# New written orders for all five engines of an attention and MoE kernel, on one core

## The chip, the core and the metric

One core of one Trainium2 chip runs the whole program. The metric is the time of one execution on the device in microseconds. The core has five engines with queues of their own: TensorE (PE), VectorE (DVE), ScalarE (ACT), GpSimd (POOL) and SyncE (SP). SP here only issues transfers; POOL and ACT issue some too. Each engine runs its own queue in order, and engines wait for each other through semaphores.

## What is computed

```python
q_bits = (np.einsum('bhsd,dk->bhsk', q, proj) > 0)          # 6 bits per row, k likewise
mask = q_bucket[:, :, :, None] == k_bucket[:, :, None, :]   # same bucket of 64
scores = np.where(mask, scale * q @ k^T, -1e9)
attn = np.exp(scores - max);  attn = attn / (attn.sum(-1) + 1e-9)
x = (attn @ v) -> (1536, 512)                               # 2 x 8 heads, 768 x 64 each
h = x @ w_in;  x = (h - np.tanh(h)) @ w_out                 # 512 -> 2048 -> 512
g = x @ w_gate;  val = x @ w_val                            # 512 -> 1536
out = (g * sigmoid(g) * val) @ w_out2                       # 1536 -> 512
```

The weights of the MoE layers come as 64-bit numbers and are turned into 32-bit ones on the chip.

## The kernel before

**Attention.** Eight pairs of heads are worked on in 12 steps each, 96 steps in all. A step takes 128 query rows of one head against all 768 keys: PE multiplies the scores into one of two score buffers `s` (L838, four matmuls of 384 columns; now and then with a one-hot matmul of the buckets ahead of it, L835), DVE takes the maximum (L848), ACT the exponential with the row sum `sm` (L850), DVE or POOL adds 1e-9 (L854), DVE takes the reciprocal `r` (L856), and POOL multiplies the 768 columns of `p` by it (L857). PE transposes `p` in two halves of three blocks (L868), and ACT or DVE copies each half out of its bank `t` into `pt` (L874). After six steps, PE multiplies `pt` by `v` in two halves (PV, L891). The scores of step n+2 need the score buffer that the exponential of step n reads. Four buffers each of `p`, `sm` and `r` go round. Hash products (L801), the splitting of the next pair's q and k into a high and a low part (L660 to L662, L757, L758), and the moves of these by SP (L748) run beside it. The program's first steps have a form of their own: ACT and POOL split and scale the first pair (L660, L662), DVE adds (L686), ACT loads its function table ahead of a one-element exponential (`warm`, L1171).

**MoE layers.** Both layers multiply 2 x 2 blocks with seven products in place of eight. A unit is 256 columns of weights by 768 rows: seven product groups of six matmuls of 384 columns (L1047). Four of a unit's banks are emptied by ACT's copy, a snap (L1027), or by DVE's add of such a copy (L1030); then come tanh or sigmoid on ACT, DVE's or POOL's subtractions and products (L964) and ACT's rounding to a high part (L969). Product banks are called `bs`, and `t`, `x` and `h` go round. An output group is six matmuls (L1101): of 384 columns in layer 1, of 512 in layer 2. It is copied to `ct` or `acc` by ACT or DVE (L1132) and added up by an accumulating transfer from POOL's queue (L1140 in layer 1, L1149 to the output in layer 2); the last two blocks of layer 2 load that sum back (L1123, SP), and DVE adds to it (L1126). A weight chunk is loaded by SP (L463), converted on DVE (L465, L468, L471), combined (L497, L499: DVE or POOL), and split by ACT (L477, L514) and DVE or POOL (L479, L516).

**What sets the order.** The code declares 3381 operations, each with what it reads and writes and with the engines that can run it; an operation's number is its place in this declaration. `ORDER` is a table with one list of numbers for each engine, and `Plan.order()` walks all five lists: an operation goes to the engine in whose list it stands, and an engine's next instruction is the next number of its list. Where an operation can run on two engines, the list in which it stands is thus the choice:

```python
op({"DVE": 0.17, "POOL": 0.3}, lambda g: g.tensor_scalar(            # L854
    out=r, in0=sm, scalar1=1e-9, scalar2=None, op0=ALU.add), r=[smk], w=[rk])
op({"ACT": 0.4, "DVE": 0.47}, lambda g, dst=dst, src=src:            # L873
   g.activation(out=dst, in_=src, func=ACTF.Copy) if g is nc.scalar else g.tensor_copy(dst, src),
   r=[("t", z)], w=[ptk + (qt, z)])
tt: op({"DVE": dve(TB), "POOL": pool(TB)} if port else {"DVE": ...}, ...)   # L964
```

Of the kernel before, what the change touches and what calls it, by code (L numbers as in the profile page):

```python
# [46 lines left out]
def chunk_keys():  # L47
# [5 lines left out]
    for i in range(NP2):  # L53
# [51 lines left out]
    """,  # L105
    DVE="""
# [1196 lines left out]
```

## Time and profile before

| | us |
|---|---|
| median of three runs | 764.66 (762.88 to 764.97) |
| the profiled execution | 764.34 |
| its span on the core | 762.3 |
| PE busy | 744.4 (98%) |
| DVE busy | 601.5 (79%) |
| ACT busy | 451.6 (59%) |
| POOL busy | 354.1 (46%) |

The granted clock is at full speed over the span. Some 2 us lie outside the span. The attention takes the first 230 us, the MoE layers the rest, and the last matmul starts at 757 us. In the rows below a time is in microseconds from the start of the span unless it is a mean or a duration marked ns. A timeline row has the start, the duration, the engine, the line and the operation, with the idle time of the engine before it and who ended it in brackets. Durations of neighbours overlap, since engines pipeline; the distance from start to start is what a step takes on its engine.

### The profile page before, as it was taken

To read this page: it belongs to the slowest core of one execution; us is meant where nothing else is said; L and a number is where in the kernel's file an instruction comes from. 1 tells how busy PE (TensorE), PEld (TensorE's weight loads), DVE (VectorE), ACT (ScalarE), POOL (GpSimd) and SP (SyncE) were. 2 spreads that over 40 slices of the span, in tenths; PEclk is the share of its full clock that TensorE was granted. 3 is DMA by queue.
4 is the path that set the end of the run, shared out by engine and by line. 5 is a ranking of instruction groups with operands and counts; after the bars stand their busy time and mean duration, and the time that the engine had idled before them with its cause. 6 is when DMAs were issued, how large, how long until landed. Compare 5 with 4: busy or idle time off the path is not lost.

```text
span 762.3 us, 12361 instructions
## 1 busy us (share of the span) xinstructions
PE 744.4 (98%) x4342; PEld 656.0 (86%) x4342; DVE 601.5 (79%) x1077; ACT 451.6 (59%) x955; POOL 354.1 (46%) x390
## 2 busy tenths in 40 slices
PE   8899999999989999999999999999999999999997
PEld 4666676766668999999999999999999998999996
DVE  6879778889888578878677789997785767789465
ACT  5787898878876556555455456665455444454230
POOL 4665667877783843123135353734235544323010
PEclk9999999999999999999999999999999999999999
DMA  6564466357123036787575764323348565587304
GB/s 173 135 191 98 128 176 167 108 131 203 52 87 108 28 68 167 180 184 191 116 186 123 203 135 106 84 97 101 108 152 194 138 130 135 127 189 160 76 15 151
DMA packets 37245, 101.09 MB, mean 133 GB/s; under 512 B 4656, under 2 KB 10160, under 8 KB 37184
## 3 DMA queue, kind: packets, MB, share of 16 engines
q1 hardware_dynamic: 28288, 71.06, 30.6%
q0 software_dynamic: 8432, 28.45, 21.2%
q10 hardware_dynamic: 464, 0.80, 0.5%
q8 instruction: 34, 0.56, 0.3%
q14 instruction: 27, 0.22, 0.1%
HBM read 49.17 MB, written 15.73 MB: 85 GB/s over the span
## 4 chain that ended last, share of the span: by engine, by line
PE 81%; POOL 6%; DVE 6%; issue 2%; DMA 2%; ACT 2%; SPq 0%; POOLq 0%; DVEq 0%; ACTq 0%
PE bs L1047 30%; PE t L1101 16%; PE h L1101 8%; PE x L891 6%; PE s L838 6%; PE x L1101 6%; PE t L868 3%; PE x L1047 2%; POOL p L857 2%; PE t L1047 2%; DVE m L848 1%; ACT p L850 1%; DMA raw<-in_kT 1%; POOL x L555 1%; PE h L1047 1%
## 5 line engine op out<-in xcount | busy, mean ns | idle before, releaser
L1047 PE MATMUL bs<-x,wi 128*128 128x384 f32 x1200 | 230.7, 335 | 1.3 <-DVE p L1030 1.3
L1047 PEld LDWEIGHTS bs<-x,wi 128*128 128x128 f32 x1200 | 210.5, 188 | 6.1 <-DVE p L1030 1.6
L857 POOL TENSOR_SCALAR p<-p,r 128x768 f32<-128x768 f32 x96 | 94.6, 989 | 25.5 <-DVE r L856 15.5
L848 DVE TENSOR_REDUCE m<-s 128x1 f32<-128x768 f32 x96 | 90.8, 952 | 14.3 <-PE s L838 13.5
L850 ACT ACTIVATE p<-s,m 128x768 f32<-128x768 f32 x96 | 86.6, 903 | 20.2 <-DVE m L848 12.1
L838 PE MATMUL s<-op 128*128 128x384 f32 x384 | 91.9, 363 | 5.1 <-ACT p L850 4.8
L1027 ACT ACTIVATE p<-bs 128x384 f32<-128x384 f32 x120 | 57.0, 490 | 54.1 <-PE bs L1047 52.7
L838 PEld LDWEIGHTS s<-op 128*128 128x128 f32 x384 | 63.7, 189 | 21.6 <-ACT p L850 12.7
L868 PEld LDWEIGHTS t<-ident,pr 128*128 128x128 f32 x576 | 59.1, 140 | 22.9 <-POOL p L857 8.0
L1101 PE MATMUL t<-op,wo 128*128 128x384 f32 x384 | 75.8, 335 | 0.0
L874 ACT ACTIVATE pt<-t 128x384 f32<-128x384 f32 x133 | 61.2, 489 | 17.7 <-PE t L868 17.2
L868 PE MATMUL t<-ident,pr 128*128 128x128 f32 x576 | 64.9, 245 | 5.5 <-POOL p L857 3.2
L891 PE MATMUL x<-pt,v 128*64 128x384 f32 x384 | 69.0, 495 | 0.0
L1101 PEld LDWEIGHTS t<-op,wo 128*128 128x128 f32 x384 | 67.2, 188 | 0.7 <-DVE ct L1132 0.3
L1101 PE MATMUL t<-wo,op 128*128 128x512 f32 x264 | 67.1, 393 | 0.0
L1140 POOL DMA_DIRECT2D acc<-ct x24 | 21.0, 887 | 78.4 <-ACT ct L1132 32.2
L1101 PEld LDWEIGHTS t<-wo,op 128*128 128x128 f32 x264 | 49.0, 188 | 8.3
L479 POOL TENSOR_TENSOR wi<-fs,wi 128x512 fp32r<-128x512 f32 (+1 forms) x25 | 39.8, 1593 | 26.0 <-ACT wi L477 25.3
L477 ACT ACTIVATE wi<-fs 128x512 fp32r<-128x512 f32 (+1 forms) x60 | 41.9, 701 | 12.5 <-DVE fs L497 4.4
L1047 PE MATMUL bs<-op,wi 128*128 128x384 f32 x240 | 47.2, 335 | 0.5 <-DVE ct L964 0.5
L891 PEld LDWEIGHTS x<-pt,v 128*64 128x64 f32 x384 | 24.7, 136 | 25.9 <-issue 23.9
L1047 PEld LDWEIGHTS bs<-op,wi 128*128 128x128 f32 x240 | 42.1, 188 | 1.4 <-DVE ct L964 1.0
(186 smaller groups left out, 1385.8 us busy)
## 6 DMA issues: line engine op xcount, KB each, us to landing
raw<-in_w SPq DMA_DIRECT2D x68, 512.0 KB, 3.6
acc<-ct POOLq DMA_DIRECT2D x24, 768.0 KB, 6.3
out<-acc POOLq DMA_DIRECT2D x12, 768.0 KB, 8.3
op<-raw SPq DMA_DIRECT2D x42, 192.0 KB, 3.2
op<-f SPq DMA_DIRECT2D x56, 96.0 KB, 3.2
v<-in_v SPq DMA_DIRECT2D x8, 384.0 KB, 3.9
out<-acc SPq DMA_DIRECT2D x4, 768.0 KB, 4.6
acc<-out SPq DMA_DIRECT2D x4, 768.0 KB, 5.3
```

What stands on the lines that cost most here:

```text
L477: op({"ACT": act(n)}, lambda e: e.activation(out=hi, in_=src, func=ACTF.Copy), r=rk, w=[wk + (0,)], due=due, late=late)
L479: op({"POOL": pool(n), "DVE": dve(n)}, lambda e: e.tensor_tensor(out=lo, in0=src, in1=hi.bitcast(F32), op=ALU.subtract), r=rk + [wk + (0,) ...
L838: g.matmul(out=s[:, kh, 0:TB], lhsT=(b, a)[first][:, q0], rhs=ks[kh][0 if first else 1], start=first, stop=not first,)
L848: op({"DVE": 0.87}, lambda g: g.tensor_reduce(out=m, in_=sv, axis=AX.XY, op=ALU.max, negate=True), r=[sk + (0,), sk + (1,)], w=[mk])
L850: op({"ACT": 0.9}, lambda g: g.activation(out=p.rearrange("p (a b) -> p a b", a=2), in_=sv, func=ACTF.Exp, bias=m, accum_out=sm), r=[sk + ...
L857: op({"POOL": 0.91}, lambda g: g.tensor_scalar(out=p, in0=p, scalar1=r, scalar2=1.0, op0=ALU.mult, op1=ALU.mult), r=[pk, rk], w=[pk])
L868: g.transpose(out=t_t[z][:, kt * 128:(kt + 1) * 128].bitcast(F32R), in_=pr[:, z * TB + kt * 128:z * TB + (kt + 1) * 128], identity=ident)
L874: g.activation(out=dst, in_=src, func=ACTF.Copy) if g is nc.scalar else g.tensor_copy(dst, src),
L891: g.matmul(out=x[r, :], lhsT=v[:, kt, r], rhs=pt_t[ptks[e][1]][:, kt, :], start=(kt == 0), stop=(kt == NKT - 1), tile_position=(0, 64 * e),)
L1027: op({"ACT": act(TB)}, lambda e: e.activation(out=dst, in_=bank(), func=ACTF.Copy), r=[bk], w=dk, due=due)
L1047: e.matmul(out=bank(), lhsT=w[:, wpart, wi * 256 + k * 128:wi * 256 + k * 128 + 128], rhs=x_at(sb, xn, xpart, k), start=first and m == 0, ...
L1101: e.matmul(out=ps(), lhsT=lhs, rhs=rhs, start=c == 0, stop=c == 5)
```

## The change

Only the table `ORDER` is written anew; everything below it is the same, 17 lines further down. So L854 of before is L871 after, L857 is L874, L1047 is L1064, L1101 is L1118.

```diff
 ORDER = {e: [int(n) for n in t.split()] for e, t in dict(
     PE="""
-        7 17 8 19 24 28 32 37 58 44 39 48 68 78 104 88 52 64 66 106 74 76 116 84 139 86 149 94 96 161 112 114
...
+        7 17 8 19 24 28 32 37 58 68 48 44 39 52 78 104 88 64 66 106 74 76 116 139 86 84 149 96 94 161
...
     ACT="""
-        0 11 12 16 15 5 29 25 22 31 27 45 40 47 60 51 70 80 65 67 90 75 77 108 129 133 118 87 141 160 159 95 151
...
+        0 11 12 16 15 25 35 27 31 22 49 45 40 60 47 51 70 55 53 80 65 67 90 77 75 108 133 129 118 87 141
...
```

The engines chosen anew, in operations of each line:

| line (before) | what | before | after |
|---|---|---|---|
| L854 | add 1e-9 to the row sum | POOL 70, DVE 26 | POOL 19, DVE 77 |
| L873 | copies of transposed halves | ACT 133, DVE 59 | ACT 118, DVE 74 |
| L757 | high part of q and k | POOL 13, ACT 1 | POOL 9, ACT 5 |
| L479 | low part of in-weights | POOL 25, DVE 35 | POOL 10, DVE 50 |
| L497 | sums of weight blocks | POOL 37, DVE 23 | POOL 7, DVE 53 |
| L516 | low part of out-weights | POOL 13, DVE 15 | POOL 2, DVE 26 |
| L555, L560 | blocks of layer 2's input | POOL 11, DVE 22 | POOL 3, DVE 30 |
| L964 | subtractions and products | POOL 53, DVE 219 | POOL 11, DVE 261 |
| L1110, L1131 | copies of output groups | ACT 106, DVE 54 | ACT 84, DVE 76 |

On POOL at the start of the attention, where `r` and `p` of four steps go round (`r_159` and `p0_87` are those of every fourth step, the next step has `r_160` and `p1_88`), there stood before:

```order
L662 TENSOR_SCALAR f_75<-fs_71 128x768
L854 TENSOR_SCALAR r_159<-sm_152 128x1
L854 TENSOR_SCALAR r_160<-sm_153 128x1
L857 TENSOR_SCALAR p3_90<-p3_90,r_162 128x768
L857 TENSOR_SCALAR p0_87<-p0_87,r_159 128x768
L857 TENSOR_SCALAR p1_88<-p1_88,r_160 128x768
L854 TENSOR_SCALAR r_161<-sm_154 128x1
L854 TENSOR_SCALAR r_159<-sm_152 128x1
L854 TENSOR_SCALAR r_162<-sm_155 128x1
L857 TENSOR_SCALAR p2_89<-p2_89,r_161 128x768
```

and there stands now, at the same place:

```order
L874 TENSOR_SCALAR p2_89<-p2_89,r_161 128x768
L871 TENSOR_SCALAR r_162<-sm_155 128x1
L874 TENSOR_SCALAR p3_90<-p3_90,r_162 128x768
L871 TENSOR_SCALAR r_161<-sm_154 128x1
L874 TENSOR_SCALAR p0_87<-p0_87,r_159 128x768
L874 TENSOR_SCALAR p2_89<-p2_89,r_161 128x768
L874 TENSOR_SCALAR p1_88<-p1_88,r_160 128x768
L874 TENSOR_SCALAR p3_90<-p3_90,r_162 128x768
```

Most adds have left POOL's queue for DVE's, and multiplies stand next to each other.

On ACT at the program's start, with the semaphores that each instruction waits for (DMAHW3 is the transfer of the first half of k into `raw`), before:

```order
L638 DMA q<-in_qT 64x768 [waits DMAHW0_49]
L1171 ACT_TABLE_LOAD
L1171 ACTIVATE warm<-warm 128x1 [waits Pool_49]
L660 ACTIVATE op<-raw 128x384 [waits DMAHW3_49,DMAHW1_49]
L660 ACTIVATE op<-raw 128x384
L660 ACTIVATE op<-f 64x384 [waits DMAHW4_49]
L689 ACTIVATE op<-s_121,csb 64x384 [waits DMASW0_49,PE_49]
```

and now:

```order
L655 DMA q<-in_qT 64x768 [waits DMAHW0_49]
L677 ACT_TABLE_LOAD [waits DMAHW3_49]
L677 ACTIVATE op<-raw 128x384 [waits DMAHW1_49]
L677 ACTIVATE op<-f 64x384 [waits DMAHW4_49]
L706 ACTIVATE op<-s_121,csb 64x384 [waits DMASW0_49,PE_49]
```

The warm-up has moved to a place some 400 operations later on ACT; the table load now belongs to the first scaling and waits for its transfer.

On PE near the end of layer 2 (`bs`, `x_108`, `t` and `h_112` are the banks, `wo` an output weight, `op_86` the slots of the middle activations), before:

```order
L1047 MATMUL bs00_2415<-x1_2606,wi_63 128x384 x6
L1101 MATMUL t_116<-wo_81,op_86 128x512 x3
L1101 MATMUL t_116<-wo_82,op_86 128x512 x3
L1047 MATMUL bs01_2419<-x1_2606,wi_63 128x384 x6
L1101 MATMUL t_117<-wo_81,op_86 128x512 x3
L1101 MATMUL t_117<-wo_82,op_86 128x512 x3
L1047 MATMUL bs00_2415<-x1_2606,wi_63 128x384 x6
L1101 MATMUL x_108<-wo_81,op_86 128x512 x3
L1101 MATMUL x_108<-wo_82,op_86 128x512 x3
```

and now:

```order
L1064 MATMUL bs00_2415<-x1_2620,wi_63 128x384 x6
L1064 MATMUL x_108<-op_86,wi_63 128x384 x6
L1064 MATMUL bs00_2415<-op_86,wi_62 128x384 x6
L1118 MATMUL t_116<-wo_81,op_86 128x512 x3
L1118 MATMUL t_116<-wo_82,op_86 128x512 x3
L1064 MATMUL bs00_2415<-x1_2620,wi_62 128x384 x6
L1118 MATMUL t_117<-wo_81,op_86 128x512 x3
L1118 MATMUL t_117<-wo_82,op_86 128x512 x3
L1118 MATMUL h_112<-wo_81,op_86 128x512 x3
L1118 MATMUL h_112<-wo_82,op_86 128x512 x3
```

Output groups, which stood one by one between products, now stand in runs, and products too; a bank such as `bs00` is filled again with one other group between. At the very end 19 output groups stand in a row, nine before. Three output groups of the fourth block of layer 2 (the last for which the sum still goes to the output by an accumulating transfer and is loaded back) stand among the last 20 groups now; before, that transfer was issued at 699.84 us.

## Rows read from the trace of the kernel before

**Rows 1.** Windows (length, then busy us of PE, weight load, DVE, ACT, POOL):

```profile
20.00:230.00 210.00, 201.34 (x1382) 143.87 (x1383) 178.54 (x348) 173.10 (x379) 150.64 (x203) 1.00 0.51 136
230.00:758.00 528.00, 526.19 (x2886) 503.00 (x2886) 408.93 (x704) 267.70 (x555) 193.72 (x167) 1.00 0.53 130
```

**Rows 2.** PE's groups, 20 to 230 us (busy us, mean ns | idle before):

```profile
L838 PE MATMUL s<-op 128*128 128x384 f32 x364 | 87.0, 363 | 3.3 <-ACT p L850 3.0
L891 PE MATMUL x<-pt,v 128*64 128x384 f32 x360 | 64.7, 495 | 0.0
L868 PE MATMUL t<-ident,pr 128*128 128x128 f32 x558 | 62.9, 245 | 5.4 <-POOL p L857 3.2 <-DVE pt L874 1.3 <-DVE r L854 0.4
...
L1047 PE MATMUL bs<-x,wi 128*128 128x384 f32 x25 | 5.3, 347 | 0.0
L801 PE MATMUL h<-fs,pj 128*32 128x384 f32 x48 | 5.1, 498 | 0.0
```

**Rows 3.** The chain that ended last (start us, us, piece):

```profile
30.64 2.09 PE x L891 x12
...
87.46 1.45 PE s L838 x8
...
498.01 1.39 PE t L1101 x6
...
753.03 2.72 PE t L1101 x12
```

**Rows 4.** Timeline of PE, 28 to 30 us:

```profile
28.34 0.97 PE L838 MATMUL s<-op 128*128 128x384 f32 x4
29.15 0.63 PE L868 MATMUL t<-ident,pr 128*128 128x128 f32 x6
29.67 0.97 PE L838 MATMUL s<-op 128*128 128x384 f32 x4
```

**Rows 5.** Timeline of POOL, 23 to 24 us:

```profile
23.68 0.21 POOL L854 TENSOR_SCALAR r<-sm 128x1 f32<-128x1 f32 x1 [1.19 <-ACT p L850]
23.98 2.99 POOL L857 TENSOR_SCALAR p<-p,r 128x768 f32<-128x768 f32 x3
```

**Rows 6.** Timeline of PE, scores into one buffer, 70 to 74 us:

```profile
70.39 0.98 PE L838 MATMUL s<-op 128*128 128x384 f32 x4 [0.20 <-ACT p L850]
...
73.58 0.97 PE L838 MATMUL s<-op 128*128 128x384 f32 x4 [0.17 <-ACT p L850]
```

**Rows 7.** Timeline of ACT at the start:

```profile
3.64 1.28 ACT L1171 ACT_TABLE_LOAD   x1 [3.64 <-DMA pj<-in_proj]
...
7.17 0.94 ACT L660 ACTIVATE op<-raw 128x384 fp32r<-128x384 f32 x2 [2.03 <-DMA raw<-in_kT]
...
9.09 1.04 ACT L689 ACTIVATE op<-s,csb 64x384 fp32r<-64x384 f32 x2 [0.44 <-PE s L695]
```

**Rows 8.** Timeline of DVE at the start:

```profile
11.62 0.91 DVE L686 TENSOR_TENSOR op<-raw,op 64x384 fp32r<-64x384 f32 x1 [0.24 <-ACT op L660]
12.46 0.94 DVE L848 TENSOR_REDUCE m<-s 128x1 f32<-128x768 f32 x1
```

**Rows 9.** Timeline of ACT and PE, 367 to 369 us:

```profile
367.69 0.49 ACT L1027 ACTIVATE p<-bs 128x384 f32<-128x384 f32 x1 [0.55 <-PE bs L1047]
...
368.53 0.85 PE L1047 MATMUL bs<-x,wi 128*128 128x384 f32 x4
```

**Rows 10.** DVE's instructions of three lines, durations (ns min/median/max; the last: mean):

```profile
L479 DVE TENSOR_TENSOR wi<-fs,wi x35: 678/695/2892, 191.2 to 705.5; 128x512 fp32r<-128x512 f32 x23, 128x768 fp32r<-128x768 f32 x12
...
L854 DVE TENSOR_SCALAR r<-sm x26: 133/144/155, 47.4 to 225.1; 128x1 f32<-128x1 f32 x26
...
L874 DVE COPY pt<-t 128x384 f32<-128x384 f32 x59 | 32.1, 550 | 5.9 <-PE t L868 5.6
```

**Rows 11.** Transfers by issuing line (count, KB each, us to landing):

```profile
out<-acc POOLq DMA_DIRECT2D x12, 768.0 KB, 8.3
...
acc<-out SPq DMA_DIRECT2D x4, 768.0 KB, 5.3
```

319 rows, old and new, of tables (ACT, DVE, PE, POOL) are left out of this document.

## The prediction

> **What bounds the kernel now.** I read the profile in this order: the windows, to see which engine is full where; then TensorE's groups by line, to see whom it waits for; then the timelines of the engine named. The windows [rows 1] show two programs. From 230 us on (both MoE layers) PE is busy 526.19 of 528.00 us, so only 1.8 us can be saved there short of less PE work. In the attention from 20 to 230 us PE is busy 201.34 of 210 us, but a busy PE also holds pipelines that drain before each wait. What PE loses I get from counting steps. A step costs what lies between two starts when nothing is waited for: a score step 0.81 us (28.34 to 29.15), a half of a transposed block 0.26 us (two in 29.15 to 29.67) [rows 4], half a PV product 2.09 us [rows 3]. The groups by line [rows 2] give 364/4 = 91 score steps, 360/12 = 30 PV halves and 558/3 = 186 transposed halves: 73.7 + 62.7 + 48.4 us, and 5.3 + 5.1 us for the two other lines there, 195.2 us. So at most 14.8 us of 210 are lost, and at least the idle that the groups show, 3.3 + 5.4 = 8.7 us. I take 14, since few one-hot matmuls are missing from the count.
>
> Whose 14 us are they? Of the 8.7 us that show, 3.2 end with POOL's multiply (L857) and 0.4 with the add for it (L854), 1.3 with DVE's copies, 3.0 with the exponential [rows 2]. POOL is late because its queue is in order: at 23.68 us it runs an add after 1.19 us of waiting for an exponential, and then three multiplies back to back (23.98, 2.99 us) [rows 5]. They had stood behind the add of a later step. In the list of before, 54 of the 96 multiplies stand behind the add of a later step. The waits for the exponential are another thing: with two score buffers, scores, maximum, exponential and the scores two steps later are a loop. One turn took 3.19 us, from 70.39 to 73.58 [rows 6], and PE waits wherever its list holds less work than that between them.
>
> **The change part by part.** Only the lists change; PE's operations and their number are the same.
>
> PE's order. A layer-2 output group takes 1.39 us when a product follows, and 1.36 us (2.72 for two) when another output group follows [rows 3]. Sixteen of the 72 are followed by one before, 58 after: 42 x 0.03 = 1.3 us less. Two score steps in a row take 1.45 us, 0.73 each against 0.81 [rows 3, 4]; 14 of them are followed by another instead of 7, 7 x 0.08 = 0.6 us. Together -1.9 us, between -1.3 (the first alone) and -2.8 (one-hot matmuls also better placed, the same 0.08 at some ten steps).
>
> The adds on POOL. 70 of the 96 adds ran on POOL, 19 do after; the multiplies behind a later step's add fall from 54 to 14. POOL's share of the loss is (3.2 + 0.4)/8.7 x 14 = 5.8 us; 40 of 54 causes gone makes -4.3 us. Ends: 0, if the loop takes the time over, and -7.5, if DVE's copies too stop being late, and only the loop's 6.5 us (24 places after, 25 before, where the list holds less than 3.19 us of PE work, short by 0.27 us on average) stay. DVE pays 51 adds and 15 copies that leave ACT: an add takes 0.13 to 0.16 and a copy 0.55 us [rows 10], 7.5 + 8.3 = 15.8 us on 178.54 of 210 [rows 1], from 85% to 92%. What hides it is that an add is short and stands after the exponential, where DVE otherwise waits; if the cover is gone, the maximum of the next step is late, and with it the loop. ACT loses the 15 copies, and so exponentials start earlier. I set these two against each other at nothing.
>
> The start. ACT's table load ran at 3.64 us, ahead of the warm-up, while ACT then idled 2.03 us for the first half of k, until 7.17 [rows 7]. The warm-up now stands some 400 operations later on ACT, so the load stands behind the wait for that transfer: ACT's first operation may come 1.28 us later. Of this 0.44 us goes into ACT's idle time at 9.09 [rows 7], and one scaling (0.47, half of the 0.94 us row) is now behind the operation that PE waits for: +0.4 us stays. Against that, the first maximum no longer stands behind the rope addition that waited for ACT (11.62, then the maximum at 12.46) [rows 8]: up to 0.8 us earlier. I take -0.3, between -0.8 and +1.3.
>
> The MoE. 106 tensor operations go from POOL to DVE and 22 copies from ACT to DVE. At 0.55 (a copy) to 0.70 us (the median of L479 on DVE) [rows 10] these are 70 to 90 us on 408.93 [rows 1]; most are of 384 columns or fewer, like the copy, so I take 70: DVE goes from 77% to about 91%, with PE full. Cost: a bank must be emptied before PE fills it again. A place is tight when PE has just one group between filling a bank and needing it again. There are 16 in the list of before; at one, ACT's copy ran at 367.69 for 0.49 us, and PE wrote into the bank at 368.53, 0.35 us after it ended [rows 9]. After, there are 65. A copy may start half an instruction late (0.28 us) and still be in time. Behind one whole instruction more it is 0.5 us late. If that is so at one place of the 49, the term is +0.5, which I take; 0 to +3 bound it (six places, or none), and more is the rival below.
> L479 on DVE takes 0.678 us at least and 2.892 at most [rows 10]: something holds it at times. The Trainium skill, "SBUF — State Buffer", section "Who interferes with whom", says that a DVE instruction with two SBUF inputs and a GpSimd instruction that reads SBUF exclude one another for the whole instruction; by that rule DVE gets time back as POOL's operations go, and the term would be 0 instead of +0.5.
>
> The tail. Three layer-2 output groups of the fourth block now run some 25 us before the end. Behind them: an accumulating DMA (8.3 us) and the load of the result back (5.3 us) [rows 11], with a copy and an add of 0.6 to 0.7, 14.9 us; PE has 12 more groups, 12 x 1.36 + 1.04 = 17.4 us. So 0, and +4 where both DMAs are slow.
>
> Sum, against the profiled run's 764.34 us: -1.9 - 0.3 - 4.3 + 0.5 = 758.34. The median of the three runs lies 0.32 above the profiled one: **758.7 us**.
>
> **The rivals.** *DVE becomes the bound* (slower). One mechanism: DVE at 91% in the MoE, in order, so that evacuations queue behind one another at the tight places, and PE stands. At every second of the 49 new places, 24 x 0.5 = 12 us: 758.34 - 0.5 + 12 + 0.3 = 770.1 us. It eats the gain from 13 such places on. For it: 65 against 16, and the fuller engine is the one that does most evacuations. Against it: 29 of the 65 go through ACT's snapshots, ACT is busy just 267.70 of 528 us [rows 1], and the 16 places of before cost nothing that shows.
> The Trainium skill, "Perfetto Trace Analysis", section "Optimizing Scalar/DVE Operations", advises moving work off a saturated DVE, even to GPSIMD; this change goes the other way, and by that rule the result is this rival's 770.1 us. The same section adds that the two share a port, so that moving work between them might not help.
>
> *The loop owns the attention* (no change). If each multiply that comes earlier only lets PE reach the wait for the exponential sooner, the 4.3 us are not seen: 758.34 + 4.3 + 0.3 = 763.0 us. For it: 3.0 of the 8.7 us are already that wait, and the places with too little work between two scores are as many after. Against it: a late multiply pushes PE's whole queue, the next scores too, so it adds to the loop's waits rather than hiding in them.
>
> *All queues fit* (larger gain). Attention -7.5, start -0.8, PE's order -1.9, and the 1.8 us of waiting in the MoE gone: 764.34 - 12.0 + 0.3 = 752.7 us.
>
> That the change does not do what it says is no case here: the lists fix engine and place of each listed operation.
>
> **How the numbers follow.** Forecast with its neighbours (758.7, tail up to +4) 0.48, larger gain 0.22, loop 0.16, DVE 0.14. What a measurement can tell from no change is 0.3%, 2.3 us: faster is below 762.4, slower above 767.0. Faster 0.48 + 0.22 = 0.70, same 0.16, slower 0.14. For 8 in 10 the range goes down to 751 (the larger gain with PE's -2.8) and up to 767, which takes in the loop and a few late evacuations, and leaves out DVE as the bound and the best ends, some 0.2.
>
> **What would show it.** PE's wait for POOL's multiply in the attention falls from 3.2 us to about 1, the wait for the exponential stays near 3: the add step is right. If the latter grows by 2 or more, the loop rival is. PE's busy time from 230 us on stays within 1 or 2 us of the window, with DVE near 90%: the MoE term is right; waits of PE's products for ACT's or DVE's evacuations, a few tenths each and dozens of them, would be the DVE rival. The table load should show just behind the k transfer at about 7.1 us, the first exponential at about 13.1. In the last 25 us a wait of PE's output groups for the final add's load would be the tail. The forecast is wrong above all if DVE's queue, fuller in both parts, delays the maxima and the evacuations more than POOL's adds did.

## The result and the profile after

The changed kernel took 769.74 us (median of four runs, 769.40 to 770.50), the kernel before 764.63: 1.0073 times as long, 95% interval 1.0055 to 1.009. The prediction was 758.7 us, 751 to 767, so the sign was wrong and the time lies 11 us above the forecast. It is close to the 770.1 us of the rival in which DVE becomes the bound, but for another reason, as the runs below show. The profiled execution took 769.86 us, with a span of 767.8. One of a_acc12's six runs below took 4069.88 us, a slow execution; the time given for it, 758.56 us, is the median of the other five (758.83 with it).

The windows of the changed kernel (length, then busy us of PE, weight load, DVE, ACT, POOL), which answer to [rows 1]:

```profile
20.00:230.00 210.00, 203.85 (x1404) 146.43 (x1404) 186.51 (x418) 172.47 (x377) 132.72 (x148) 1.00 0.53 137
230.00:758.00 528.00, 519.98 (x2842) 498.41 (x2841) 440.09 (x823) 252.04 (x528) 71.90 (x63) 0.99 0.51 125
```

In the attention PE does more in the same 210 us. From 230 us on it misses 8.0 of 528 us, where it missed 1.8. The view of PE's waits (what waited for what: us in total, times, longest) shows at once that these are two waits and not dozens:

```profile
PE bs L1064 <- DVE p L1047: 4.7, 1, 4.7
PE bs L1064 <- ACT p L1044: 3.3, 1, 3.3
PE s L855 <- ACT p L867: 2.2, 4, 0.7
PE x L734 <- DMA q<-in_qT: 2.1, 1, 2.1
...
PE t L885 <- POOL p L874: 0.4, 1, 0.4
```

Both lie in layer 2, at 648 and 687 us. The engines named there, ACT and DVE, are late because ACT itself stood, until 644.91 and until 685.89 us. ACT, DVE and PE around the first one, from the timeline (start, duration, engine, line, operation, idle before with its releaser):

```profile
644.91 1.08 ACT L1149 ACTIVATE acc<-t 128x512 f32<-128x512 f32 x2 [3.85 <-DMA out<-acc]
...
647.39 0.50 ACT L1044 ACTIVATE p<-bs 128x384 f32<-128x384 f32 x1
...
647.93 0.56 DVE L1047 TENSOR_TENSOR p<-bs,p 128x384 f32<-128x384 f32 x1 [3.61 <-ACT p L1044]
...
647.95 3.10 PE L1064 MATMUL bs<-x,wi 128*128 128x384 f32 x12 [3.32 <-ACT p L1044]
```

ACT's copy of an output group into a staging buffer (L1149) waits 3.85 us for an accumulating transfer (L1166, L1149 of before) that still reads that buffer. The snap (L1044) that PE needs stands behind the copy and four more pieces of ACT's work, and starts at 647.39. The second one:

```profile
685.89 0.87 ACT L1044 ACTIVATE p<-bs 128x384 f32<-128x384 f32 x2 [5.78 <-POOL ct L981]
...
686.41 0.56 DVE L1047 TENSOR_TENSOR p<-bs,p 128x384 f32<-128x384 f32 x1 [4.91 <-ACT p L1044]
...
687.03 3.83 PE L1064 MATMUL bs<-x,wi 128*128 128x384 f32 x12 [4.70 <-DVE p L1047]
```

Here ACT waits for a product on POOL (L981, L964 of before). POOL's timeline holds the cause of both:

```profile
627.04 1.30 POOL L1166 DMA_DIRECT2D out<-acc  x1 [7.32 <-ACT acc L1149]
636.25 1.30 POOL L1166 DMA_DIRECT2D out<-acc  x1 [7.91 <-issue]
637.07 1.53 POOL L981 TENSOR_TENSOR op<-ct,op 128x384 fp32r<-128x384 f32 x1
645.20 1.29 POOL L1166 DMA_DIRECT2D out<-acc  x1 [6.61 <-issue]
...
674.59 1.29 POOL L496 TENSOR_TENSOR wi<-fs,wi 128x512 fp32r<-128x512 f32 x1 [1.45 <-ACT wi L494]
675.82 1.29 POOL L1166 DMA_DIRECT2D out<-acc  x1
683.55 1.28 POOL L1166 DMA_DIRECT2D out<-acc  x1 [6.43 <-issue]
684.36 1.49 POOL L981 TENSOR_TENSOR ct<-p,ct 128x384 f32<-128x384 f32 x1
691.16 1.30 POOL L1166 DMA_DIRECT2D out<-acc  x1 [5.31 <-DVE fs L514]
```

The transfers to the output follow at 7.6 to 9.2 us where they are close, and one takes 7.3 to 8.9 us to land: where POOL stands ahead of one with "issue", it is issued when the one before has landed. The list of after has them late and in bunches. The one issued at 636.25 us had its data ready at 593.0 (the end of the last copy into its buffer), but stands behind one whose data came at 626.6. The one issued at 675.82 had its data at 650.0, and stands behind two weight subtractions that came at 671.3 and 674.6. The bunch behind it then holds the product at 684.36, whose inputs were there at 673.2.

After each wait PE also runs slower. The windows at 648 and 687 us (columns as above; the first figure behind POOL's is the granted clock) and four pieces of the chain, the first of which is the transfer that held ACT's copy until 644.9:

```profile
648.00:650.00 2.00, 2.00 (x10) 2.00 (x11) 1.97 (x4) 1.89 (x5) 0.00 (x0) 0.83 1.08 176
650.00:652.00 2.00, 2.00 (x7) 1.80 (x6) 1.35 (x3) 0.43 (x2) 0.00 (x0) 0.50 1.16 213
...
687.00:689.00 2.00, 1.97 (x6) 1.98 (x7) 2.00 (x4) 0.00 (x0) 0.00 (x0) 0.50 1.10 201
```

```profile
636.25 8.63 DMA out<-acc
...
647.95 3.10 PE bs L1064 x12
651.05 2.22 PE t L1118 x6
...
687.03 8.02 PE bs L1064 x36
```

A product takes 1.04 us and an output group 1.36, so PE's three pieces took 1.0, 0.9 and 1.8 us too long, 3.7 us together. That is PE at the lower of its two clock levels (granted 0.50, from 649.3 to 652.7 and from 686.9 to 690.3 us) after it had stood 3.3 and 4.7 us. The waits thus cost 8.0 + 3.7 = 11.7 us by this count. Set against a_acc12 below, which has the same order on PE, it is a little less: from the first output group of layer 2 to the last the changed kernel takes 258.1 us (504.18 to 762.31), a_acc12 248.9 (501.73 to 750.58), 9.3 less, with 1.0 us of such waits left.

### The profile page after: what moved, and what is told of

Same layout as the page of the kernel before. It is cut to its first block, busy times and chain, and to the rows that moved or that the text cites. A ratio compares the mean times of both kernels' runs of the same rounds, so it can differ in the third digit from the quotient of the medians.

```text
span 767.8 us, 12261 instructions
## 1 busy us (share of the span) xinstructions
PE 744.3 (97%) x4342; PEld 659.0 (86%) x4342; DVE 642.6 (84%) x1271; ACT 436.0 (57%) x925; POOL 211.7 (28%) x226
## 4 chain that ended last, share of the span: by engine, by line
PE 82%; DVE 4%; DMA 4%; issue 4%; ACT 2%; SPq 2%; POOL 2%; ACTq 0%; POOLq 0%; DVEq 0%
PE bs L1064 31%; PE t L1118 16%; PE h L1118 8%; PE s L855 6%; PE x L908 6%; PE x L1118 6%; PE t L885 4%; PE x L1064 2%; DVE m L865 2%; DMA op<-f 2%; SPq L765 2%; PE t L1064 2%; ACT p L867 1%; DMA out<-acc 1%; PE h L1064 1%
## 5 line engine op out<-in xcount | busy, mean ns | idle before, releaser
L1064 PE MATMUL bs<-x,wi 128*128 128x384 f32 x1200 | 229.4, 338 | 8.0 <-DVE p L1047 4.7
L1064 PEld LDWEIGHTS bs<-x,wi 128*128 128x128 f32 x1200 | 211.4, 189 | 11.0 <-DVE p L1047 5.0
L874 POOL TENSOR_SCALAR p<-p,r 128x768 f32<-128x768 f32 x96 | 92.5, 969 | 54.9 <-DVE r L873 27.7
L1044 ACT ACTIVATE p<-bs 128x384 f32<-128x384 f32 x120 | 57.6, 492 | 76.5 <-PE bs L1064 69.4
L1118 PE MATMUL t<-op,wo 128*128 128x384 f32 x384 | 75.4, 334 | 0.0
L1118 PEld LDWEIGHTS t<-op,wo 128*128 128x128 f32 x384 | 67.2, 188 | 0.2
L1118 PE MATMUL t<-wo,op 128*128 128x512 f32 x264 | 65.5, 394 | 0.0
L891 ACT ACTIVATE pt<-t 128x384 f32<-128x384 f32 x118 | 55.0, 489 | 17.7 <-PE t L885 16.6
L1118 PEld LDWEIGHTS t<-wo,op 128*128 128x128 f32 x264 | 50.1, 191 | 10.2 <-ACT acc L1149 0.2
L1064 PE MATMUL bs<-op,wi 128*128 128x384 f32 x240 | 47.8, 334 | 0.0
L891 DVE COPY pt<-t 128x384 f32<-128x384 f32 x74 | 40.1, 549 | 7.8 <-PE t L885 7.6
L1166 POOL DMA_DIRECT2D out<-acc x12 | 15.6, 1299 | 103.4 <-issue 46.1
```

What stands on the lines that cost most here:

```text
L874: op({"POOL": 0.91}, lambda g: g.tensor_scalar(out=p, in0=p, scalar1=r, scalar2=1.0, op0=ALU.mult, op1=ALU.mult), r=[pk, rk], w=[pk])
L1044: op({"ACT": act(TB)}, lambda e: e.activation(out=dst, in_=bank(), func=ACTF.Copy), r=[bk], w=dk, due=due)
L1064: e.matmul(out=bank(), lhsT=w[:, wpart, wi * 256 + k * 128:wi * 256 + k * 128 + 128], rhs=x_at(sb, xn, xpart, k), start=first and m == 0, ...
L1118: e.matmul(out=ps(), lhsT=lhs, rhs=rhs, start=c == 0, stop=c == 5)
```

## The experiments

Theory A was: the order of the accumulating transfers on POOL makes both waits. Theory B was the prediction's rival: DVE is at its limit and evacuations miss the tight places. All kernels here have only `ORDER` edited; their lines are numbered 8 above those of the kernel before (b_late 7). Diffs show the piece of the list.

**a_acc1, a_acc2 and a_acc12: four transfers forward.** a_acc1 has the first edit, a_acc2 the second, a_acc12 both. The transfers moved are 2783, 2874, 2949 and 2980; the first of them is the one issued at 636.25 us, the third the one at 675.82.

```diff
     POOL="""
...
-        2708 2737 2814 3010 2903 2783 2972 2874
+        2708 2737 2783 2814 3010 2874 2903 2972
...
-        3180 3182 2949 3040 3136 2980 3253
+        2949 2980 3180 3182 3040 3136 3253
```

> The changed kernel, with two of layer 2's accumulating transfers moved forward in POOL's list: the first block's third one (2783, whose data lay ready at 593.0 us but which was issued at 636.25) ahead of 2814, and 2874 (ready at 616.3, issued at 645.20) ahead of 2903. Theory A, POOL's accumulating transfers go one after another (each is issued 0.3 us after the one before has landed) and two that come too late hold a staging buffer that ACT wants to write, so that ACT stands 3.85 us and PE 3.32 us: the stall at 647.9 us is gone, and with it the lower clock behind it, so 3.5 to 5 us less than the changed kernel's 769.7, 765 to 766; the stall at 687 us stays. Theory B, DVE at its limit: the stalls come from evacuations that queue, and moving two transfers leaves them; 769 to 770.

> The changed kernel, with two other accumulating transfers moved forward in POOL's list: 2949 (data ready at 650.0 us, issued at 675.82 behind two weight subtractions) and 2980 (ready at 656.7, issued at 691.16), both ahead of those two subtractions. Theory A: transfer 3040 no longer stands at POOL's head until the one before has landed, the product (3136) behind it runs when its inputs are there, and ACT and PE don't wait 5.8 and 4.7 us for it; the stall at 687 us is gone with the lower clock behind it, 5 to 7 us less, 763 to 765; the stall at 647.9 us stays. Theory B: 769 to 770, with a stall of about the same size at another place.

> The changed kernel with both edits to POOL's list, four accumulating transfers moved forward, all engines chosen as in the changed kernel. Theory A: neither stall is left, some 11 us less than 769.7: 758 to 760, faster than the kernel before by 0.6 to 0.9%, which is what the prediction had for the rest of the change. Theory B: 767 or more.

Measured: a_acc1 763.91 us (0.9997 of before, 0.9987 to 1.0008), a_acc2 763.28 (0.9988, 0.9969 to 1.0008), a_acc12 758.56 (0.9936, 0.9914 to 0.9957). Each edit takes 5.8 to 6.5 us off the changed kernel's 769.7, both together 11.2: the result goes from slower than before to faster, with every engine chosen as the change has it. In their profiles each edit removes its own wait and leaves the other: 4.6 us at the second in a_acc1, 2.5 at the first in a_acc2. Of PE's waits for its banks this is left in a_acc12:

```profile
PE bs L1055 <- DVE p L1038: 1.0, 2, 0.6
```

That is 1.0 of the 8.0 us. Theory A holds, in sign and about in size (a_acc1 gains 1 us more than it expected). Single runs of a_acc2 spread from 759.40 to 767.00 us and those of a_sub below from 759.57 to 766.08; the profile is of the fastest of the former and of the slowest of the latter, so their waits can't be set against the medians.

**a_sub: the transfers as they are, one product ahead of one.** It tells the queue from the buffers.

```diff
     POOL="""
...
-        2949 3040 3136 2980
+        2949 3136 3040 2980
```

> The changed kernel, with one thing exchanged in POOL's list: the product 3136 of layer 2, which stood behind the accumulating transfer 3040, goes ahead of it. Every transfer keeps its place. Theory A (POOL's queue stands at a transfer that has to wait for the landing of the one before, and what stands behind it is late): 3136 runs at about 677 us instead of 684.4, ACT's snap and DVE's add and so PE no longer wait 4.7 us; 5 to 7 us less than 769.7, 763 to 765, though the transfers go as before. If it was the late transfers themselves (their buffers) that held PE at 687 us, the stall stays: 769 to 770.

Measured: 764.2 us (0.9990, 0.9973 to 1.0007), 5.5 less than the changed kernel. POOL and ACT there:

```profile
677.00 1.29 POOL L1157 DMA_DIRECT2D out<-acc  x1
...
677.82 1.52 POOL L972 TENSOR_TENSOR ct<-p,ct 128x384 f32<-128x384 f32 x1
677.98 0.49 ACT L1035 ACTIVATE p<-bs 128x384 f32<-128x384 f32 x1 [1.88 <-DVE op L972]
```

The product runs at 677.82 instead of 684.36, and the second wait is gone, although the transfers go as late as before the edit. So the second wait was POOL's queue. The first one, which stays here (3.8 us), was a buffer by ACT's row at 644.91; b_late tests that.

**b_late: the kernel before, with the late order of two transfers alone.**

```diff
     POOL="""
...
-        2783
...
-        2874 3015 2903 2941
+        3015 2903 2783 2874 2941
```

> The kernel before, with only the order of six accumulating transfers of layer 2 as the changed kernel has it: 2783 and 2874 go behind 2903 on POOL. Nothing else is changed, engines and PE's order are those of before. Theory A: 2783's data lies from 588 us on, but it is now issued when 2903 has landed, about 632 us, and lands at about 641; ACT's copy into the same buffer, at 631.1 us before, waits until then, and PE behind it: one stall of 4 to 9 us near 633 to 642 and the lower clock after it, 769 to 774. Theory B (DVE's load and the runs of output groups make the stalls): nothing of these is changed, 764 to 765.

Measured: 774.78 us (1.0143, 1.0119 to 1.0168), 10.3 more than before.

```profile
633.74 1.28 POOL L1156 DMA_DIRECT2D out<-acc  x1 [6.42 <-issue]
...
640.99 0.60 ACT L1139 ACTIVATE acc<-t 128x512 f32<-128x512 f32 x1 [10.93 <-DMA out<-acc]
641.06 0.69 DVE L1139 COPY acc<-h 128x512 f32<-128x512 f32 x1 [10.18 <-DMA out<-acc]
...
641.81 2.93 PE L1108 MATMUL h<-wo,op 128*128 128x512 f32 x6 [9.53 <-DVE acc L1139]
```

The kernel before, with its own engines and PE order, gets the wait in the same way. It is longer, 9.5 us: ACT and DVE both stand at copies into buffers of the late transfers, from 630.1 and 630.9 us on. PE's last row here runs 2.93 us instead of 1.55: the slower clock again. The late order is enough by itself to make such a wait.

**a_dve: the rival's load, beyond what the change does.** The last 33 tensor operations of the MoE part go from POOL to DVE.

```diff
     POOL="""
...
+        2708 2737 2783 2814 2874 2903 2949 2980 3040 3069 3115 3146
...
     DVE="""
...
-        3129 3184 3097 3245
+        3129 3184 3136 3097 3245
```

> The changed kernel with the four transfers moved forward, and the last 33 tensor operations that the MoE part has on POOL put on DVE too, each at the place in DVE's list that answers to its time; POOL there only issues transfers. Theory A: DVE's load goes from 84% to 87 or 88% between 230 us and the end, and nothing waits for it: 758 to 760, as with the four transfers alone. Theory B (DVE is near its limit, so that evacuations miss the tight places): each further operation costs about as much as the 128 moved ones would, 33 x 0.3 = 10 us, 765 to 769.

Measured: 769.31 us (1.0061, 1.0040 to 1.0082), some 10.8 more than a_acc12, as theory B expected of it. The three largest of PE's waits from 230 us on, and the windows from 230 us on of a_acc12 and of a_dve:

```profile
PE bs L1055 <- DVE p L1038: 2.4, 3, 1.1
PE t L1109 <- DVE op L972: 1.8, 1, 1.8
PE bs L1055 <- DVE op L972: 1.4, 1, 1.4
```

```profile
230.00:758.00 528.00, 521.00 (x2854) 497.45 (x2852) 442.79 (x823) 250.68 (x524) 71.13 (x63) 1.00 0.53 131
```

```profile
230.00:758.00 528.00, 520.74 (x2855) 496.26 (x2855) 453.95 (x853) 252.90 (x530) 36.27 (x36) 1.00 0.51 125
```

(a_acc12's window ends behind its last matmul, a_dve's does not, so their PE columns can't be set side by side.) With DVE busy 442.79 us PE waits 1.0 us for it; with 453.95 it waits 6.6 us, and up to more than a whole instruction at a time. But that is not DVE at its limit. The windows of a_acc12, and then of a_dve, where a_dve loses most and where its DVE is fullest:

```profile
400.00:500.00 100.00, 100.00 (x577) 99.54 (x576) 94.01 (x172) 57.33 (x115) 18.51 (x16) 1.00 0.55 135
```

```profile
400.00:500.00 100.00, 96.64 (x549) 94.58 (x548) 91.20 (x170) 54.64 (x111) 7.81 (x9) 1.00 0.58 143
500.00:600.00 100.00, 99.43 (x531) 93.42 (x530) 95.62 (x181) 49.06 (x100) 2.61 (x2) 1.00 0.40 119
```

From 400 to 500 us PE loses 3.4 us in a_dve with DVE busy 91.20, less than in a_acc12, where PE loses none; from 500 to 600 us, with DVE at 95.62, it loses 0.6. I put the 33 operations where DVE's list was at their time, without reordering what stood there. So the windows speak for their places in DVE's queue rather than for their number; no run with other places was made. Theory B has the size right, and its cause is not shown. Not all of the loss is there: the profiled a_dve starts layer 1's first output group at 244.11 us and a_acc12 at 239.02. Six of the 33 run ahead of 230 us, but the changed kernel, a_acc1, a_acc2 and a_sub, whose lists are the same as a_acc12's up to there, start it anywhere from 238.45 to 241.43, so part of these 5 us is no effect of the edit.

**b_adds and a_addsback: the adds on POOL.** b_adds makes this part of the change alone, a_addsback undoes it alone.

```diff
     POOL="""
-        1 4 20 2 49 33 35 102 42 61 53 71 63 73 81 55 83 91
+        1 4 20 2 49 33 35 102 42 61 53 63 73 55 83 91
...
     DVE="""
...
-        62 79 72 34 89 105 82 107
+        62 79 71 72 34 89 105 81 82 107
```

```diff
     POOL="""
-        1 29 20 33 4 2 42 61 63 102 73 100 83 91 93
+        1 29 20 33 4 2 42 61 71 63 102 81 73 100 83 91 109 93
```

> The kernel before with one part of the change alone: the 56 adds of 1e-9 that the change puts on DVE and that were on POOL go to DVE, each just ahead of its reciprocal; all else is as before. Theory C, the adds in POOL's queue cost the attention most of what POOL's waits show: PE's wait for POOL's multiply falls from 3.2 us to 1 or less, 3 to 4.5 us less than before, 760 to 762. Theory D, the loop of scores, maximum, exponential and next scores takes the time over: PE's wait for the exponential grows by what the other loses, and the time stays at 764 to 765.

> The changed kernel with the four transfers moved forward, and the 56 adds that the change took from POOL put back into POOL's queue, 55 of them ahead of the multiply of the step before, as most stood in the kernel before; the rest of the attention keeps the new lists. Theory C (the adds in POOL's queue are the cost): PE's wait for POOL's multiply comes back to some 3 us and the time goes from 758.8 up by 3 to 4.5, 762 to 763. Theory D (the loop of scores, maximum and exponential covers most of it, as the 1.2 us of the adds moved alone say): 759 to 760.5, and the rest of the attention's gain belongs to the new order of the other operations.

Measured: b_adds 763.15 us (0.9989, 0.9977 to 1.0000), a_addsback 771.51 (1.0104, 1.0086 to 1.0121). In b_adds PE's groups from 20 to 230 us, to be read against [rows 2], are:

```profile
L846 PE MATMUL s<-op 128*128 128x384 f32 x364 | 87.1, 363 | 3.7 <-ACT p L858 3.6
...
L876 PE MATMUL t<-ident,pr 128*128 128x128 f32 x558 | 63.0, 244 | 3.5 <-POOL p L865 1.8 <-DVE pt L882 0.9 <-DVE r L862 0.4
```

The wait for POOL's multiply falls from 3.2 to 1.8 us, that for the exponential rises from 3.0 to 3.6: moved alone, the adds bring about 1.2 us, which can't be told from none. Theory D was nearer. But put back into the new lists they cost some 13 us, three to four times what theory C expected, and all of it in the attention: layer 1's first output group starts at 252.54 us. The largest of PE's waits there is

```profile
PE t L876 <- POOL p L865: 6.8, 10, 2.1
```

So neither size held. An add that stands ahead of an earlier step's multiply does hold POOL, as the prediction had it. It costs much in the new lists and little in the old ones, so its cost belongs to no one part of the change. In a_addsback 55 of the 56 stand that way, and 69 multiplies stand behind a later step's add (54 in the kernel before, 6 in b_adds), which makes its number an upper one.

**a_warm and a_best: the start, and a few adds of DVE.** Both build on a_acc12; a_best holds a_warm's edit too.

```diff
     ACT="""
-        0 11 12 16 15 25 35 27
+        0 11 12 16 15 5 25 35 27
...
     DVE="""
...
-        3173 3000 3171 3174 3175 3105 3176 3177 3178 3126 3127
+        3173 3000 3105 3171 3174 3175 3126 3176 3177 3178 3127
```

> The changed kernel with the four transfers moved forward and ACT's warm-up back at the place that it has in the kernel before, right behind the first transfers (and POOL's memset for it ahead of the scalings): the start of before, undone alone. The table load runs at 3.6 us again, and ACT's first scaling at 6.3 instead of 7.5. If the table load behind the transfer of k is what costs the start its time, 0.8 to 1.3 us less than with the four transfers alone, 757.5 to 758; if PE waits for q's transfer at 9.8 us anyway, within 0.4 of 758.8.

> The changed kernel with the four transfers moved forward and ACT's warm-up at its early place, and four of DVE's operations moved in DVE's list of layer 2: the adds 3105, 3126, 3097 and 3227, which empty banks, go ahead of the weight conversions and subtractions behind which they stood while their inputs lay ready (3105 ran at 663.43 us with its inputs there at 660.8). PE waited 1.3 and 0.7 us for two of them. If that is all, 1 to 2 us less than 758.2: 756 to 757.5. If the converted weights then come late in turn, 758 or more.

Measured: a_warm 758.21 us (0.9917, 0.9899 to 0.9934), a_best 757.62 (0.9925, 0.9913 to 0.9938). Against a_acc12's 0.9936 the intervals overlap, and by their ratios to the runs of before the two are even: neither edit shows an effect. All three beat both kernels, by 0.6 to 0.8% the one before.

## Why the prediction was wrong

The sum had five terms, the tail (0) among them. The one that failed is the MoE's: it priced evacuations on a fuller DVE, and put the order of POOL's accumulating transfers at nothing.

- **PE's order** (-1.9) held in its larger part, as far as its price goes; no run has it alone. Output groups in a row do take 1.36 us each after the change, as this piece of the chain at the end shows:

```profile
757.03 4.08 PE t L1118 x18
```

- **The attention** (-4.3) came out in the right size, by a mixed cause. From 20 to 230 us these are PE's groups of the changed kernel:

```profile
L855 PE MATMUL s<-op 128*128 128x384 f32 x364 | 85.0, 360 | 2.1 <-ACT p L867 1.7
...
L885 PE MATMUL t<-ident,pr 128*128 128x128 f32 x565 | 63.9, 246 | 3.9 <-ACT pt L891 1.1 <-DVE pt L891 1.1 <-DVE r L873 1.0
...
L1064 PE MATMUL bs<-x,wi 128*128 128x384 f32 x39 | 8.0, 346 | 0.0
```

  Against [rows 2] PE gets 14 matmuls further into the first product groups and 7 transposed blocks further: 14 x 0.173 + 7 x 0.087 = 3.0 us gained. The same lists in a_acc12's execution gained 5.2 us (52 product matmuls and 564 blocks). POOL's multiply hardly shows as a wait any more (0.4 us in all, from 3.2). That it was the adds' leaving by itself was wrong: alone they bring about 1.2 us, and what in the new lists brings the rest no run separates. The term was also too large by its own working. It took few one-hot matmuls to be missing from the count of steps, but there are 27 in that window of the kernel before:

```profile
L835 PE MATMUL h<-bits,fs 128*128 128x384 bf16 x27 | 9.1, 337 | 0.0
```

  At 0.173 us each, the price of a product's matmul, they take 4.7 of the 14.8 us that were left over; then about 10 us are lost and not 14, and the term would have been -3.1.
- **The start** (-0.3) was near nothing, as taken, but not by the path given. The table load did run behind the k transfer, at 6.25 us and not at 7.1, and the first exponential at 12.88, ahead of the 13.1 named. The first PV product starts at 30.50 us, and at 30.58 before, so none of it is left by then. PE stood 2.06 us for q ahead of 9.79 us, and was granted 0.52 from 11 to 12 (1.00 before); that these two took what the earlier exponential gave is not shown. a_warm, which undoes the move of the table load, can't be told from a_acc12.

```profile
6.25 1.28 ACT L677 ACT_TABLE_LOAD   x1 [6.25 <-DMA raw<-in_kT]
```

```profile
9.79 0.51 PE L734 MATMUL x<-q,pj 64*32 64x384 f32 x2 [2.06 <-DMA q<-in_qT]
```

```profile
11.00:12.00 1.00, 1.00 (x6) 1.00 (x5) 0.72 (x3) 1.00 (x3) 0.40 (x1) 0.52 1.06 412
```

- **The MoE** (+0.5, 0 to +3) is the step that failed. I looked for the price of denser work in the evacuations by ACT and DVE, and counted tight places. Those cost nothing: from 230 to 640 us PE is busy 410.00 of 410 us. What cost the 11.7 us was POOL's queue, which I had counted for weight and activation work but not for layer 2's 12 accumulating transfers. With 8.3 us each [rows 11] they hold 100 of the 190 us from the first to the end, one after another, and the view of before has them at 574 to 700 us. Their new places in POOL's list were in the list of after to be read: two of them behind operations that could not run for another 25 to 34 us. The prediction gave one such transfer, the last, a term (the tail, 0 to +4). That term was right, nothing waited there. The same sum was not made for the other eleven.
- **DVE's load** was taken as 91%, and came out as 440.09 of 528 us, 83%: 31 us more than before, not 70. DVE's own subtractions became shorter, at most 0.954 us where they had taken up to 2.892 [rows 10]:

```profile
L496 DVE TENSOR_TENSOR wi<-fs,wi x50: 679/685/954, 226.8 to 715.6; 128x512 fp32r<-128x512 f32 x34, 128x768 fp32r<-128x768 f32 x16
```

  Most of the gap between 70 and 31 is time that DVE got back: for as many instructions of the same line and shape as before, it took about 28 us less. The rest is overlap of neighbours, which a busy time counts once. The Trainium skill, "SBUF — State Buffer", section "Who interferes with whom", has a DVE instruction with two SBUF inputs contend with a GpSimd instruction that reads SBUF, for ports that one of them holds as an exclusive lock. By that rule DVE gets time back when POOL's operations leave, and the trace is in line with it.

Without the failing step the sum was good: a_acc12, which has the whole change but for the places of four transfers, took 758.56 us against the 758.7 forecast. That it agrees to 0.1 us is luck in part: a_acc12's interval is 0.9914 to 0.9957 of the kernel before, 757.8 to 761.0 us, and the attention's term was too large by its working and had the wrong cause. Of the rivals, the one with the right number (DVE as the bound, 770.1) had the wrong mechanism: a_acc12 keeps DVE's load and loses the waits. The Trainium skill, "Perfetto Trace Analysis", section "Optimizing Scalar/DVE Operations", says that moving work off a saturated DVE, even to GPSIMD, may make sense. The change went the other way, with DVE busy 83%, and no cost of that shows; a_dve's loss lies at single operations and not where DVE is fullest, so these runs don't bear the rule out. What I would call wrong in the odds is that no case with a place and a price stood for POOL's transfers in the middle of layer 2.

The texts ahead of the result also say that the warm-up moved some 400 operations down ACT's list; it is 206. No number hangs on it.

## What to carry to other kernels

When a list of operations is written anew, go through every queue for the operations that block it: for each transfer that has to wait for the one before, compare when its data is ready with what stands ahead of it, and name what waits for its buffer and what stands behind it. A few such operations, 4 of 3381 here, turned a gain of 0.6% into a loss of 0.7%, and engine loads show nothing of it. And a part of such a change may have no price of its own: here the adds were worth 1.2 us in the old order and some 13 in the new one.

## What the runs showed of the hardware

Accumulating transfers of 768 KB to the output went one at a time. Each took 7.3 to 8.9 us to land, and one that stood right behind another in POOL's queue was issued 0.3 us after the other had landed: the one issued at 636.25 us landed at 644.88, and the next was issued at 645.20. Those into SBUF in layer 1 overlapped: they took 5.7 us or more to land, and these two were issued 1.9 us apart:

```profile
276.57 0.93 POOL L1157 DMA_DIRECT2D acc<-ct  x1 [11.19 <-ACT ct L1149]
...
278.48 1.21 POOL L1157 DMA_DIRECT2D acc<-ct  x1
```

What makes the former go singly is open. The profile names nothing that POOL waited for ahead of them ("issue"), and the program itself orders two such transfers only where they go to the same rows of the output. And a wait of PE of 3 to 5 us costs more than it shows: at its end or just behind it the granted clock was 0.50 for some 3 us, both times, which added 3.7 us to 8.0.
